# A new order table, and register loads as operations of their own, in a two-layer attention and expert kernel

## The chip, the cores and the metric

One Trainium2 chip, one of its cores. The core has five engines with queues of their own: TensorE (PE) multiplies, VectorE (DVE), ScalarE (ACT) and GpSimd (POOL) work on elements, SyncE (SP) issues transfers. Each engine runs its instructions strictly in the order in which the program lists them, and the engines wait for one another through semaphores. The metric is the device time of one execution in microseconds (us), lower is better.

## The reference

The input x has 2048 rows of 512 numbers (bf16). Two layers run one after the other, each as "x plus f(layernorm(x))" on these two functions:

```python
qkv = x @ wqkv                       # 32 heads of 16
phi = lambda t: where(t > 0, t + 1, exp(t)) + 1e-6
kv, z = sum_s phi(k) v, sum_s phi(k)
o = (phi(q) kv) / (phi(q) z + 1e-6)  # linear attention
A = o @ wo
...
r = x @ w_r                          # one score for each row
B: the 2 rows with the highest score go through silu(g @ w_gate) * (g @ w_up) @ w_down,
   are scaled by the sigmoid of their score and added back; the other 2046 rows pass through
```

The program has this A, B, A, B: attention on all rows, the expert for two chosen rows, and both again. Which two rows are chosen is known only at run time, so their indices are loaded from memory into engine registers, and copies, additions and the last transfers use these registers as addresses.

## The kernel before

The 2048 rows are 16 tiles of 128, each a [128, 512] block in SBUF. The kernel first records all its work, of both layers, as operations: each has an engine, a function that issues its instructions, and the values that it reads and writes. A string named `ORDER`, two characters for each operation, says in which order they are issued; a string `PICK` of letters (A, D, P) says which engine takes those operations that ACT, DVE or POOL could do. Nothing is reordered afterwards, so these strings are the queues. The planner's durations beside each operation (`dve(0.61, ...)`) were used when the strings were made; when the kernel is built they decide nothing. PSUM is shared out in three pools: "mm" of 3 buffers, "g" of 4 and "tp" of 1; an operation that wants a buffer waits until the reader of that buffer's last content is through.

The steps that the texts below speak of, with the line numbers before:

- **Start.** `stats` (L334, L335) is the mean and variance of a tile on DVE, `stats_act` (L348, L351) makes 1/deviation (`rho`) on ACT, L874 is a copy of a PSUM value (`wl`) on ACT, L876 (`wkc`) on DVE, L421 and L415 are the first products of keys on PE, L433 adds a tile's key-value product.
- **Side chain.** While layer 1's last tiles and layer 2's first are under way, the two chosen rows are found (L991 on PE, L996 to L1007 on DVE, which packs both indices into `pw`), loaded into POOL's registers (L1024, `load_idx`), copied out of `xn` (L1098), transposed (L1111) and put through the expert (L1069 to L1214). The second pair of loads (POOL at L1277, DVE at L1302) comes before the rows are put back.
- **Layer 2's output.** L586 is the output product, L591 adds it to x on DVE, L663 in `lin(j)` computes the score's linear part from four tiles at once (j = 0 to 3), read by DVE at L675.
- **Tail.** L681 and L684 make scores, L991, L996, L1370, L1376, L1429, L1445, L1457 and L1459 find the two best rows, L1464 makes selection weights `WL`, L1475 and L1483 select and transpose, L1491 makes `xs`, L1500 and L1540 are the expert, L1553 casts its result `yo`, L1003 and L1007 pack the indices, `regs` loads them on ACT and SP (L1024), and L1557 writes the two rows over the output. L323 and L321 make the other rows' output (`pk`), which L1360 stores in four transfers of 512 KB; the two last rows wait until all four have landed, since they overwrite rows of them.

When the operations are issued, GpSimd's that are marked `port=True` are made to wait for the last DVE instruction of that mark ahead of them in the table:

```python
if o.port and o.eng == "DVE":
    held = mine[-1]
elif o.port and held is not None:
    tc.add_manual_dep(mine[0], held.name, ...)
```

Of the kernel before, what the change touches and what calls it, by code (L numbers as in the profile page):

```python
# [28 lines left out]
ORDER = (
    "8c3y8d00010X0Y8b0302050k3z060708090P0Q0R048a0Z0a0b0S0W0V0c0T3x0U0l0e8Z0f45460g0y0w0r0i0m0h0x0n0o0z0j0p0A1I0B1D17"  # L30
    "0s0C0D1K0t101C110u12181J0v191a1U1T131L1F151b1M0E0H1E1l1c1d1A1G1B1N221e1O1Z1R1H1V421W1f1X0F1g1r1m282E2G1Y23241s1n"
    "2F1h1P1t2H1u1o2A1q2P291v251p2B26432Z2I271w341x2J2K1j0G2C2R0d2l2D3E2L2a2m0I0q2U2b2j142N162V2Q1y2k2u2S363G352T2n37"
    "2W2c0J3H2d2X401S3F2w302Y2v2e0K2f314C3Z2o2x2p3220332y2g2h2s3I3J1i2i1k383j4D3a2z3b2M3c1Q3V2O3K3N3d3P3k3l3m2q3p3W3Q"
    "3X3Y39444J3S3U4E3r3n3q4F3s3R4K3t3L4L0L3A4G8X4M4H3T413f3e3B3g3o3u3v3w4N4I3C3h1z214O4z3D4R3i4P504S514r4Q0M4d534T8Y"
    "523O4s544e4f4v4w0N4t4u552r4U2t564x4k4l3M4m4g4h4V4W4y4X4Y4j4i4748494b4c4Z4a4n4o4q575V5W58595X4A5Z4p5a5b5E5F5G5Y5S"
    "5A5B5T5U5L5M5N5O5P5D5H5o5C5p5q5r5Q5c5d5R5I6B685s5t5u5e5v6C0O5w6P5n5x5J5y6D6062665f5K6I6Q6J755g6469766R5h6X8W5i6r"
    "6W6s6y5j6z6A6K6Y5k775m617C636Z6a5l6b6c6E656L706F6M7D6d6e6f7K6G677n7o6H6t6g6N6h6j7E7u7v6S6T6n6l7p6OAC7J7LAD6p7M8P"
    "8QAE7N8I8J7O826U7w7P6u6v7Q7R8R6V83AI8K817S8f84AJA06k6w857T8gA57U6x6mAK7Y86AL7a788e7971877A888h5z8i7B6o7c89AA8j8k"
    "728A6q737W8l748B7q7r7sAM8CAgAFAh8m7V7tAi8n8E8o6i4B8p8qAB7Z8D8G7FAj7b997GAsAu8rAHAtAN7d7H7IAkAv7X8t7e7f7g7h7i9o9p"
    "9q9r7x7j8L7y7z8MAaAc80Ab7k8F8N8H7l8u8OA6A7Aw8v8s8x8w8y7mAd8z8S8T90AUAW92AG91A8A993948UAT9PAV98959Q9AAZ9B9s9C9w8V"  # L40
    "979tAX9D9u9xAf9E9y9FAe9zA19vAl9L9R9SA2A39M9H9N969G9O9I9J9K9W9TAr9UA49V9X9YAxAy9Z9aAYAmAoAn9b9dAOAP9c9eAz9f9g9hAp"
    "AqB79iB8B0AQB1BSAR9k9j9lB9B2BU9nBHBAASBRBIBJ9mCEBKBLBTB3BVBWB4B5BMBBCFBXBOCHCGBCB6BjC2BNBkBFBlBYBDC3CIBPBbBdBfBG"
    "C4CaC5BeBZBmBqBEBaBxBrBsBzBhByBnBcBQBgBtC6CRBuCJBiBpBoCdCSC0CTC1C7CKC8BvCeCOCLCWCZCXC9CMBwCYCUCfCbCgCcCsCNChCiCP"
    "CVCQCtCvCuCACjCwCyCBDACzDPCxCkCDClD0D1DBDQCmDCCnDJDMDRCoCpDDCCDFDKDND2DLDGDODEDnDHDTD3DSCrD4CqD6DUDqDrD5DtDeDoD8"
    "DuD7D9DVDWDXDfDsDpEAEBDvEMDgDaDZENDxDIECEJDyEWDwDbEKEODzDYE0DhEXDiDjDkE3DlELEYEZDmEaEQEbErE1EREsE2EPEDEtESE4EGEd"
    "EuEEEFEHEIE6EcEvEUETF0EeExEVEgEfEmEwEyEhF2DcF1DdEnF3EoEpE8EqEzEiF7E7F8EkE5EjE9FHElF9FAF5FGFKFLF4F6FIFJFBFDFNFUFC"
    "FEFRFFFMFOFPFSFQFTFVFW"
)
# [79 lines left out]
def linear_attention_moe(  # L128
# [1176 lines left out]

    def f():
# [325 lines left out]
```

## Time and profile before

| | |
|---|---|
| time, median of 3 runs | 155.57 us (155.18 to 155.70) |
| the profiled execution's own time | 155.52 us |
| its span in the trace | 153.7 us |
| mean granted clock of TensorE | 0.979 of full speed |
| PE busy | 145.5 us (95%) |
| DVE, ACT, POOL busy | 124.2, 115.8, 43.6 us (81%, 75%, 28%) |

The span is the trace's first to last record. The execution's own time is 1.8 us longer. An engine's busy time says only how often it had something to do; what an edit is worth is read at the place where it stands, from what ends the wait of whoever is waited for.

### The profile page before, as it was taken

Reading aid. Unit: us, or ns where it says so; the run is one execution under the profiler, and the core shown is the slowest. Engines: PE = TensorE matmul, PEld = TensorE weight load, DVE = VectorE, ACT = ScalarE, POOL = GpSimd, SP = SyncE. Lnnn points to the kernel's source line nnn. Section 1 sums busy time; section 2 is a strip of 40 time slices with the busy share of each in tenths; the row PEclk is TensorE's granted clock in tenths of the full one; section 3 lists DMA queues with packets and bytes.
Section 4 is the critical chain, followed back from the end, with each engine's and each line's share of the span. In section 5 each row is a group of like instructions: output and inputs, shape, how many; then the busy total and the mean of one; then the engine's idle time right before and its main releaser. Section 6 shows DMA issues by size and latency. Waiting matters only on the chain.

```text
span 153.7 us, 3661 instructions
## 1 busy us (share of the span) xinstructions
PE 145.5 (95%) x1257; PEld 71.7 (47%) x1257; DVE 124.2 (81%) x446; ACT 115.8 (75%) x276; POOL 43.6 (28%) x108
## 2 busy tenths in 40 slices
PE   7799999999999999999999999999999999995891
PEld 2344444444445444444444455445464454552480
DVE  1599998977469899999999698953759999899920
ACT  3389999888188899998899474355688988899920
POOL 7725640113000224007100002320325104786300
PEclk9999999999999999999999999999999999999965
DMA  4999999899895000531535400000000000030660
GB/s 124 349 308 389 301 234 202 113 261 346 354 384 235 0 4 0 102 37 34 105 70 95 97 17 0 4 2 0 4 0 4 0 0 0 4 136 4 210 204 1
DMA packets 23154, 18.19 MB, mean 118 GB/s; under 512 B 18016, under 2 KB 20576, under 8 KB 22752
## 3 DMA queue, kind: packets, MB, share of 16 engines
q1 hardware_dynamic: 22840, 17.57, 42.3%
q10 hardware_dynamic: 296, 0.39, 0.8%
q8 instruction: 9, 0.15, 0.4%
q14 instruction: 9, 0.07, 0.2%
HBM read 11.67 MB, written 2.10 MB: 90 GB/s over the span
## 4 chain that ended last, share of the span: by engine, by line
PE 73%; DVE 13%; ACT 5%; DMA 3%; issue 2%; POOL 1%; POOLq 0%; ACTq 0%
PE g L433 18%; PE mm L448 16%; PE mm L401 9%; PE g L586 9%; PE mm L415 9%; DVE x L591 5%; DMA x<-in_A_x_dram 3%; ACT e L370 1%; PE tp L546 1%; PE g L529 1%; PE g L1500 1%; DVE pk L323 1%; ACT rl L373 1%; PE mm L562 1%; PE mm L1069 1%
## 5 line engine op out<-in xcount | busy, mean ns | idle before, releaser
L370 ACT ACTIVATE e<-mm 128x512 bf16<-128x512 f32 x48 | 28.4, 598 | 10.3 <-PE mm L401 6.3
L448 PE MATMUL mm<-xnT,wq 128*128 128x512 bf16 x128 | 31.9, 379 | 0.0
L433 PE MATMUL g<-pk,xn 128*128 128x512 bf16 x128 | 31.1, 379 | 0.0
L586 PE MATMUL g<-KW,pq 128*128 128x512 bf16 (+2 forms) x132 | 30.0, 373 | 0.0
L606 ACT ACTIVATE sq<-x 128x512 bf16<-128x512 bf16 (+2 forms) x31 | 18.9, 609 | 1.3 <-DVE x L591 0.7
L433 PEld LDWEIGHTS <-xn 128*128 128x128 bf16 x128 | 12.4, 99 | 14.6 <-issue 0.3
L586 PEld LDWEIGHTS <-pq 128*128 128x128 bf16 x132 | 12.3, 98 | 13.7 <-DVE pq L570 0.3
L448 PEld LDWEIGHTS <-wq 128*128 128x128 bf16 x128 | 11.7, 98 | 12.8
L374 DVE TENSOR_SCALAR em<-e 128x512 bf16<-128x512 bf16 x48 | 14.1, 294 | 4.2 <-ACT e L370 4.0
L401 PE MATMUL mm<-wk,xnT 128*128 128x512 bf16 x64 | 15.8, 379 | 0.0
L415 PE MATMUL mm<-wkc,xt 128*128 128x512 bf16 x60 | 14.5, 379 | 0.0
L334 DVE BATCH_NORM_STATS2 st<-x 128x6 f32<-128x512 bf16 x16 | 10.4, 676 | 3.6 <-DMA x<-in_A_x_dram 3.6
L373 ACT ACTIVATE rl<-mm 128x512 bf16<-128x512 f32 x16 | 9.4, 594 | 3.2 <-PE mm L448 3.1
L591 DVE SCALAR_TENSOR_TENSOR x<-x,opr,g 128x512 bf16<-128x512 bf16 (+2 forms) x17 | 11.5, 708 | 0.1
L388 ACT ACTIVATE e<-mm,rho 128x512 bf16<-128x512 f32 x16 | 10.9, 687 | 0.7 <-PE mm L421 0.4
L570 POOL TENSOR_TENSOR pq<-pq,rd 128x1024 bf16<-128x1024 bf16 x2 | 4.2, 2079 | 24.3 <-DVE wor L846 15.2
L591 DVE SCALAR_TENSOR_TENSOR x<-x,g 128x512 bf16<-128x512 bf16 x16 | 10.7, 682 | 0.5 <-PE g L586 0.2
L389 ACT ACTIVATE rl<-mm,rho 128x512 bf16<-128x512 f32 x16 | 10.7, 689 | 0.5 <-PE mm L415 0.5
L381 DVE SCALAR_TENSOR_TENSOR pk<-mm,em 128x512 bf16<-128x512 f32 x16 | 10.9, 685 | 0.1
L381 DVE SCALAR_TENSOR_TENSOR pq<-mm,em 128x512 bf16<-128x512 f32 x16 | 10.8, 686 | 0.2
L323 POOL TENSOR_SCALAR xn<-x,rho,nb 128x512 bf16<-128x512 bf16 x9 | 6.8, 767 | 12.9 <-DVE em L374 4.5
L415 PEld LDWEIGHTS <-xt 128*128 128x128 bf16 x64 | 6.2, 98 | 7.5 <-issue 0.2
(297 smaller groups left out, 243.0 us busy)
## 6 DMA issues: line engine op xcount, KB each, us to landing
wgu<-in_B_wgu_dram SPq DMA_DIRECT2D x2, 1408.0 KB, 8.1
out_dram<-pk SPq DMA_DIRECT2D x4, 512.0 KB, 3.0
wd<-in_B_wd_dram SPq DMA_DIRECT2D x1, 1408.0 KB, 6.6
xt<-in_A_xt_dram SPq DMA_DIRECT2D x2, 512.0 KB, 7.7
x<-in_A_x_dram SPq DMA_DIRECT2D x2, 512.0 KB, 9.4
xt<-in_A_xt_dram SPq DMA_DIRECT2D x3, 256.0 KB, 4.4
x<-in_A_x_dram SPq DMA_DIRECT2D x3, 256.0 KB, 4.5
wq<-in_A_wq_dram SPq DMA_DIRECT2D x1, 512.0 KB
```

Source lines behind the costliest of these rows:

```text
L370: act(0.5, lambda: A.activation(out=e()[:], in_=p()[:], func=ACT.Exp), r=[p], w=[e], **k)
L373: act(0.5, lambda: A.activation(out=rl()[:], in_=p()[:], func=ACT.Relu), r=[p], w=[rl], **k)
L374: dve(0.2, lambda: V.tensor_scalar(out=em()[:], in0=e()[:], scalar1=1.0, scalar2=TINY, op0=ALU.min, op1=ALU.add), r=[e], w=[em], port=True ...
L381: dve(0.6, lambda: V.scalar_tensor_tensor(out=out_ap, in0=p()[:], scalar=0.0, in1=em()[:], op0=ALU.max, op1=ALU.add), r=[p, em], w=[key], **k)
L388: act(0.57, lambda: A.activation(out=e()[:], in_=p()[:], func=ACT.Exp, scale=s_), r=[p, ("rho0", t)], w=[e])
L401: T_.matmul(p()[:], lhsT=xnT[:, c, t * P : (t + 1) * P], rhs=wk[:, c, :], start=(c == 0), stop=(c == NC - 1))
L415: T_.matmul(p()[:], lhsT=xt[:, t, c, :], rhs=w_[:, c, :], start=(c == 0), stop=(c == NC - 1 and not raw))
L433: T_.matmul(Gs[c]()[:], lhsT=xn[:, t, gcol(c) : gcol(c) + P], rhs=pk[:, t, :], start=first, stop=last)
L448: T_.matmul(p()[:], lhsT=wq[:, i, c, :], rhs=xnT[:, i, j * D : (j + 1) * D], start=(i == 0), stop=(i == NC - 1))
L586: T_.matmul(p()[:, 0:n], lhsT=pqt(c, t * P, P), rhs=KWs[layer][:, c, a : a + n], start=(c == 0), stop=(c == NC - 1),)
L591: dve(0.07 + 0.6 * n / D, lambda a=a, n=n, p=p, h=h: V.scalar_tensor_tensor(out=x[:, t, a : a + n], in0=x[:, t, a : a + n], scalar=1.0 if ...
L606: A.activation(out=sq()[:, 0:n], in_=xh, func=ACT.Square, scale=float(D) ** -0.5, accum_out=acc)
```

## The change

The strings `ORDER` and `PICK` are replaced (966 operations in place of 963; here the first line of each):

```diff
 ORDER = (
-    "8c3y8d00010X0Y8b0302050k3z060708090P0Q0R048a0Z0a0b0S0W0V0c0T3x0U0l0e8Z0f45460g0y0w0r0i0m0h0x0n0o0z0j0p0A1I0B1D17"
...
+    "8b00010P048Z8X8Y030X028c0Q050k0607080Y090R0A0B0C0D0E0S0Z0a8a0V0H0W0F0U3x0T0l0e0G0f0h45460b0c0w0g0y0m0n0i0r0z0s17"
...
 def lin(j):
-        p, lo = ps("tp", [P, NJ, 2]), NJ * j
+        p, lo = ps("mm" if j == NC - 1 else "tp", [P, NJ, 2]), NJ * j
...
+    def load_i():
+        IV["i"], IV["t"] = load_idx(ENG.Pool, pw1)
+    pool(1.1, load_i, r=["pw"], w=["ld0"], lat=0.02)
+
     def gather():
-        IV["i"], tv = load_idx(ENG.Pool, pw1)
         for j in range(2):
-            G_.tensor_copy(out=xsel[:, j : j + 1, :], in_=xn[:, bass.ds(tv[j], 1), 0:D])
-    pool(2.2, gather, r=["pw"] + [("xn", t) for t in range(NT)], w=["xsel"], port=True)
+            G_.tensor_copy(out=xsel[:, j : j + 1, :], in_=xn[:, bass.ds(IV["t"][j], 1), 0:D])
+    pool(1.2, gather, r=["ld0"] + [("xn", t) for t in range(NT)], w=["xsel"], port=True)
...
+    def load_h():
         IV["h"] = load_idx(ENG.Pool, B["ph"], S // 2)[0]
+    pool(1.1, load_h, r=["ph"], w=["ld1"], lat=0.02)
...
+        if j == 0:
+            def load_v():
+                IV["v"] = load_idx(ENG.DVE, pw1)[1]
+            dve(0.9, load_v, r=["pw"], w=["ld2"], lat=0.02)
+
         def f(j=j, pp=pp):
-            if j == 0:
-                IV["v"] = load_idx(ENG.DVE, pw1)[1]
...
-        pl.any(first({"POOL": (0.8, False), "DVE": (0.25, True)}, eng), f,
+        pl.any(first({"POOL": (0.75, True), "DVE": (0.25, True)}, eng), f,
...
-        pl.any({"POOL": (0.55, False), "DVE": (0.27, True)}, f,
+        pl.any({"POOL": (0.5, True), "DVE": (0.27, True)}, f,
...
-           r=[("xo", t) for t in range(lo, hi)], w=[("out", lo)], lat=2.6).kb = 96.0 * (hi - lo)
+           r=[("xo", t) for t in range(lo, hi)], w=[("out", lo)], lat=2.1).kb = 96.0 * (hi - lo)
...
-    pool(0.3, f, r=["g8e", "eyg"], w=[("key", 1, NT)])
+    pool(0.42, f, r=["g8e", "eyg"], w=[("key", 1, NT)], port=True)
```

So three register loads are operations of their own, which the table can place; the last `lin` takes its PSUM buffer from "mm"; the True and False are the `port` marks, which now stand on GpSimd's small operations on scores too (`last_scales`, `halves`, and the key of L1438); the rest of the numbers are the planner's. PE's queue has 2490 rows before and after, with the same products. In the changed file the lines stand 1 to 10 further down.

Three places show how the table moves instructions. The first is SP's queue at the end of the program. L1360 (L1370 in the changed file) stores the output `pk`, L1024 (L1025) is the load of the first chosen row's index, L1557 (L1567) stores that row. Before:

```order
L1360 DMA out_dram<-pk 128x4x512 x4
L1024 TENSOR_LOAD s_194
L1024 ISA x2
L1557 REGISTER_ALU
L1557 ISA
L1557 DMA out_dram<-yo 4x128
```

Now:

```order
L1370 DMA out_dram<-pk 128x4x512 x3
L1025 TENSOR_LOAD s_194
L1025 ISA x2
L1370 DMA out_dram<-pk 128x4x512
L1567 REGISTER_ALU
L1567 ISA
L1567 DMA out_dram<-yo 4x128
```

The fourth store has moved behind the register load, which waits for the packed indices `s_194`. The second place is DVE's queue from the selection weights `WL` to the expert's input, where `s_194` is made (L1007, now L1008). Before:

```order
L1464 SCALAR_TENSOR_TENSOR WL<-keys,s_192,sc 128x45 x2
L1003 TENSOR_SCALAR s_193<-s_192 128x2
L1007 SCALAR_TENSOR_TENSOR s_194<-s_193 128x1
L323 TENSOR_SCALAR pk<-x,opr,nb 128x512 x3
L1491 TENSOR_REDUCE xs_145<-tp 128x4x2
L1491 TENSOR_REDUCE xoT<-tp 128x4x2
```

Now:

```order
L1474 SCALAR_TENSOR_TENSOR WL<-keys,s_192,sc 128x45 x2
L323 TENSOR_SCALAR pk<-x,opr,nb 128x512 x4
L1501 TENSOR_REDUCE xs_145<-tp 128x4x2
L1501 TENSOR_REDUCE xoT<-tp 128x4x2
L323 TENSOR_SCALAR pk<-x,opr,nb 128x512
L1004 TENSOR_SCALAR s_193<-s_192 128x2
L1008 SCALAR_TENSOR_TENSOR s_194<-s_193 128x1
```

The two operations that pack the indices have moved from ahead of `xs` to behind it, with one output tile more ahead of them. The third place is the start of ACT's queue. Before:

```order
L348 ACTIVATE lnv<-mv,eps_t 128x1
L351 ACTIVATE rho<-lnv 128x1
L874 ACTIVATE wl<-g 128x512
L321 ACTIVATE xn<-x,nb,rho 128x512
L388 ACTIVATE e<-mm,rho 128x512
```

Now:

```order
L967 ACTIVATE mask_102<-mask_103 128x512
L875 ACTIVATE wl<-g 128x512
L349 ACTIVATE lnv<-mv,eps_t 128x1
L352 ACTIVATE rho<-lnv 128x1
L390 ACTIVATE rl<-mm,rho 128x512
L389 ACTIVATE e<-mm,rho 128x512
```

`wl` has moved ahead of the first tile's statistics, and that tile's `xn` has left ACT (for POOL).

## Rows read from the trace of the kernel before

**Rows 1.** The page: the chain that ended last, share of the span by engine.

```profile
PE 73%; DVE 13%; ACT 5%; DMA 3%; issue 2%; POOL 1%; POOLq 0%; ACTq 0%
```

**Rows 2.** Timeline of PE, side chain: start us, us, engine, line, tiles, count.

```profile
92.07 0.38 PE L991 MATMUL tp<-identf,s 128*128 128x128 f32 x2
...
95.96 1.03 PE L433 MATMUL g<-pk,xn 128*128 128x512 bf16 x4
96.82 0.34 PE L1111 MATMUL tp<-ohm,xsel 128*128 128x2 bf16 x8
...
97.89 1.03 PE L433 MATMUL g<-pk,xn 128*128 128x512 bf16 x4
98.84 1.49 PE L1069 MATMUL mm<-wgu,xs 128*32 128x384 bf16 x32
100.26 2.76 PE L433 MATMUL g<-pk,xn 128*128 128x512 bf16 x12
```

**Rows 3.** Timeline of the start: at a row's end, idle time before it and its releaser.

```profile
6.74 0.58 ACT L874 ACTIVATE wl<-g 128x512 bf16<-128x512 f32 x1
...
7.35 1.43 DVE L876 TENSOR_TENSOR wkc<-wk,wl 128x512 bf16<-128x512 bf16 x4 [0.21 <-ACT wl L874]
7.37 1.02 PE L421 MATMUL mm<-wl,xt 128*128 128x512 bf16 x4 [0.75 <-ACT wl L874]
...
8.50 2.87 PE L415 MATMUL mm<-wkc,xt 128*128 128x512 bf16 x12
```

**Rows 4.** Timeline of PE, the last outputs and scores.

```profile
137.91 0.54 PE L663 MATMUL tp<-KWr,pq 128*128 128x2 bf16 x16
138.31 0.49 PE L586 MATMUL g<-KW,pq 128*128 128x192 bf16 x4
139.62 0.54 PE L663 MATMUL tp<-KWr,pq 128*128 128x2 bf16 x16 [0.82 <-DVE s L675]
...
141.39 0.43 PE L991 MATMUL tp<-identf,s 128*128 128x128 f32 x2 [0.78 <-DVE s L675]
```

**Rows 5.** Timeline of DVE, the same stretch and the tail.

```profile
139.48 0.40 DVE L591 SCALAR_TENSOR_TENSOR x<-x,opr,g 128x192 bf16<-128x192 bf16 x1
...
144.44 0.51 DVE L1464 SCALAR_TENSOR_TENSOR WL<-keys,s,sc 128x45 bf16<-128x45 f32 x2
...
145.13 1.05 DVE L323 TENSOR_SCALAR pk<-x,opr,nb 128x512 bf16<-128x512 bf16 x3
146.10 0.17 DVE L1491 TENSOR_REDUCE xs<-tp 128x8 bf16<-128x16 f32 x1
...
150.42 0.29 DVE L1553 CAST yo<-g 128x128 bf16<-128x128 f32 x1 [1.14 <-PE g L1540]
```

**Rows 6.** SP's queue from the fourth store; under it all four stores' landing.

```profile
146.25 0.37 SPq L1360 DMA_DIRECT2D out_dram<-pk  x1
150.73 0.70 SPq L1557 DMA_DIRECT2D out_dram<-yo  x1
...
DMA to landing us min/median/max: 3.0/3.0/3.9
```

**Rows 7.** Timeline of POOL, the copy of the chosen rows.

```profile
95.01 1.23 POOL L1098 COPY xsel<-xn 128x512 bf16 x2 [20.02 <-DVE s L1059]
```

**Rows 8.** Timeline of PE where layer 1's rows are put back.

```profile
114.56 0.22 PE L494 MATMUL g<-pk4m,V 128*128 128x128 bf16 x1
114.90 0.41 PE L546 MATMUL tp<-pq,Z 128*32 128x128 bf16 x16
```

**Rows 9.** Register loads by their line: duration ns min/median/max, first and last start.

```profile
L1024 SPq TENSOR_LOAD <-s x1: 497/497/497, 146.7 to 146.7; - x1
...
L1024 SPq SEQ_ASSERT  x1: 33/33/33, 147.5 to 147.5; - x1
```

**Rows 10.** Timeline of POOL: one small operation beside a pass of VectorE, and alone.

```profile
131.90 0.71 POOL L1341 TENSOR_SCALAR opr<-rho 128x4 f32<-128x4 f32 x1 [0.81 <-ACT rho L351]
...
135.60 0.22 POOL L1341 TENSOR_SCALAR opr<-rho 128x4 f32<-128x4 f32 x1
```

More of the change, by code (lines that the diff above doesn't have):

```diff
@@ L29 @@
 ORDER = (
-    "8c3y8d00010X0Y8b0302050k3z060708090P0Q0R048a0Z0a0b0S0W0V0c0T3x0U0l0e8Z0f45460g0y0w0r0i0m0h0x0n0o0z0j0p0A1I0B1D17"
[L31 to L44, printed above, removed]
@@ L45 @@
-    "DuD7D9DVDWDXDfDsDpEAEBDvEMDgDaDZENDxDIECEJDyEWDwDbEKEODzDYE0DhEXDiDjDkE3DlELEYEZDmEaEQEbErE1EREsE2EPEDEtESE4EGEd"
-    "EuEEEFEHEIE6EcEvEUETF0EeExEVEgEfEmEwEyEhF2DcF1DdEnF3EoEpE8EqEzEiF7E7F8EkE5EjE9FHElF9FAF5FGFKFLF4F6FIFJFBFDFNFUFC"
-    "FEFRFFFMFOFPFSFQFTFVFW"
+    "8b00010P048Z8X8Y030X028c0Q050k0607080Y090R0A0B0C0D0E0S0Z0a8a0V0H0W0F0U3x0T0l0e0G0f0h45460b0c0w0g0y0m0n0i0r0z0s17"
+    "0x0o100j0d0u0t3y1I1K0p3z1D110q0I120v151c1L1J19131a1E8d1F161C18141d1M1b1N1G281A421B1e0J1T1O1U431V1H1X1t0K1l1W1m1n"
@@ new lines @@
+    "1f2G1P292H1Z221Y2A1q2Z1u1r232E1s1v1w1R1g241Q1j1o251p1h2a2F27442I1x262B2P2j2J2K2c2b2C2D2U203E2Q3F2u2R2f3G2w3H0L2l"
+    "342v3I2V2g1i402L2k1y2x352e2d2S2m2h362y2n2W372i2X2o3Z2Y3J3a2N1k1S3b2p212T1z4C2q2s3P30383K3Q3A3R3S3N3j313T323c332z"
+    "3B3C3d3D3p4J3l3k3m3q3n3L3r0M392M4D3s3f2O4E4K3g4F3U3e3o3t3u3v4L3h413i3O4G3w2t3V4N4M4O4R4H3W4I4r4P4S4Q4d4s534t4T3X"
+    "4u543Y4U4e4v2r554f4k4V4g4w4b560N4x4h3M4y4l4z4m4j4c504Z4X515H524W4a4i5I4Y5O5J4n574o585K5E5P5S594p5F5A5Q4q5G5B5T5U"
+    "5R5L5M5Z5a5D5n5V5N5b5W5o5C5p5X475q5r5c5Y5s485d5t5u5e5f6P5v5w755x5y766I6J5g0O8W6Q5h685i69776B6K5j6R60615k626C6y7C"
@@ new lines @@
+    "66646z6X6D5l6r6A5m6Y63706Z6a7D6E6s6b67497K6c7J8P6d6F6G8Q6W657E6t8I6e6H6f6g6L6M7u4A7L7M6h8J6l8R7N7v6n6NAD8f7O6O6S"
+    "7n8K7PAP8gAE6j6TAF8h7Q7R8e6o7o7w8i6p6u6k7SAQ82A17TAR6m6q6U7U8j6V7a7p6v838k5z8l7FA67Y7cAS8485866w81717b877d8mAB8n"
+    "7G8o6x884BAJ7H728p7W8973AC7I8A7Z788r747V8tAK8B8CALAT8E8G6i8qAb7X9p797AAc9q8DAG7BAdAM9rAIAN7q9AAe7e8s7f7gAf7h9s7r"
+    "7s8FAO7i7tAH7x7y7j7k7l7m7z8S8T8L808U8v8V8M8H8N8OAn8xAoAq8u8w8y8z909192AtApAh939499959QAu9xAvAiAj9y9EA29BAU9C969R"
+    "Aa9z9798A3A09F9DA4AgAk9G9M9IAw9N9J9K9O9P9S9H9T9XAm9LA5BE9U9VA7Ar9W9YAV9tB7A89Z9a9b9u9vA9As9wAX9c9d9eAyAx9f9gAz9h"
@@ new lines @@
+    "B09i9jB49kAWB3B59mAABKBMAlAYB6B99nBAC59lBIC7BLBJCdB1AZ9oB2C6BNBOBBC0C8BUBYBPB8BXBCBZBVC1C3BmC2CHBQBnBoBWBaBSBDCI"
+    "BtC4CJCMBRBuBvCNC9BbBpBeCKCOBFBTBqBwCPBrBsBxCABgBhCBBzCQBcBGBfBiCjBHBjBkCUBdCkCRCLClCyCvBlCZByCmCVCSCcCXCWCTCYCg"
+    "CCCbCzD0CnCwChCDCxCECaCeD2DPCiD1DDCfCGCoD3D4D5CpCFDSCqDEDQD6DFDMCrDGDRDTDBCsDJDUDADNDVDWDOCuCtDXDHD7DtD8D9DuDwDq"
+    "DYDhDxEZDZDvDaDyDrDsEPDbDiDIEaEbDjDzE0EDEQEcDcDKE1EdEuEREMDLEvEEDdE2E3DkENEeDmDlDnDoEwETDpEGEIEJEFEOEHEKESE4ELDC"
+    "ExE5EyF0EXEgEfEhEjEUEVEzE6EWEiE7DfF1F2EYEqErEsEkF3DeF5F4FAEpEtFBElF6EmEnE9FKEoFCEBEAF7FLDgE8F9FDFEFFF8FGFNFHFUFJ"
@@ L48 @@
+    "FOFPFQFRECFIFSFTFVFWFXFMFYFZ"
 )
@@ L63 @@
 PICK = (
-    "DDDDADPDPPDDPDPPDDAPDDPPDDPDDDADDDDDAADAAAAADDDAPDADDAAAAADDPPAAPAAAAPPAPPAAAAPADDDDAPDADADDADDPPPDDDDPDAADAAADD"
-    "DDADDDPAPDPDADADADDAADPPPDPAAAAADPPPPPAAAAAPPPADDAAAADAAAPPDPDADD"
+    "DDDDPDPDPPDDPPPDDDPPDDPPDDDDDDPDDPDPAADDAAAADDDADPADDAAAAADDDPPPPAAAAPDPDPAAAADADDDADDDDAAPPADDDDDDDDDDDADDAAAAD"
+    "DDADDDDADDDDAPAPADDAADPPPAPPAAAADPPPPAAAAAAPDPAADDAAADAAADDDPDDAD"
 )
@@ L333, in stats @@
         st = sb("st", [P, V.BN_STATS_DIM], FP32)
-        dve(0.61, lambda: V.bn_stats(out=st()[:], in_=x[:, t, :]), r=[("x", t)], w=[st]).early = 4.0
+        o = dve(0.61, lambda: V.bn_stats(out=st()[:], in_=x[:, t, :]), r=[("x", t)], w=[st])
+        o.early, o.avail = (None, 5.4) if t == 0 else (4.0, 0.0)
         dve(0.1, lambda: V.bn_aggr(out=mv[:, 0, t, :], in_=st()[:]), r=[st], w=[("mv0", t)])
@@ L1258, in f @@
             G_.tensor_copy(out=xnT[:, :, bass.ds(IV["i"][j], 1)], in_=xc4[:, :, 2 + j : 3 + j])
-    pool(0.5, f, r=["xc4"], w=[("xnT", t) for t in range(NT)], port=True)
+    pool(0.5, f, r=["xc4", "ld0"], w=[("xnT", t) for t in range(NT)], port=True)
     qp, qe, pqx = ps("tp", [P, NC, 2]), small([P, NC, 2]), small([P, NC, 2], BF16)
@@ L1272, in linear_attention_moe @@
     dve(0.25, f, r=["qe", qp], w=["pqx"], port=True)
+    def load_h():
+        IV["h"] = load_idx(ENG.Pool, B["ph"], S // 2)[0]
+    pool(1.1, load_h, r=["ph"], w=["ld1"], lat=0.02)
     def f():
-        IV["h"] = load_idx(ENG.Pool, B["ph"], S // 2)[0]
         for j in range(2):
             G_.tensor_copy(out=pqs[0][:, :, bass.ds(IV["h"][j], 1)], in_=pqx[:, :, j : j + 1])
-    pool(0.5, f, r=["pqx", "ph"], w=[("pq", j, c) for j in range(NJ // 2) for c in range(NC)], port=True)
+    pool(0.5, f, r=["pqx", "ld1"], w=[("pq", j, c) for j in range(NJ // 2) for c in range(NC)], port=True)
     pl.bias = 4.0
@@ L1296, in linear_attention_moe @@
            r=["s2", "yw"], w=[pp])
+        if j == 0:
+            def load_v():
+                IV["v"] = load_idx(ENG.DVE, pw1)[1]
+            dve(0.9, load_v, r=["pw"], w=["ld2"], lat=0.02)
         def f(j=j, pp=pp):
-            if j == 0:
-                IV["v"] = load_idx(ENG.DVE, pw1)[1]
             xv = x[:, bass.ds(IV["v"][j], 1), :]
             V.tensor_tensor(out=xv, in0=xv, in1=pp()[:], op=ALU.add)
-        dve(0.7 + 0.9 * (j == 0), f, r=[pp], w=[("x", t) for t in range(NT)])
+        dve(0.62, f, r=[pp, "ld2"], w=[("x", t) for t in range(NT)])
     vp, vb = ps("tp", [P, 2]), small([P, 2])
```

## The prediction, made before the changed kernel ran

> **What bounds the kernel now.** I read the chain that ended last first, then the timelines at its ends and wherever it leaves TensorE. The chain is TensorE's for 73% of the span [rows 1]. From about 8.5 us on, PE issues one 128x512 matmul after another, and four of them take 0.86 us from start to start (95.96 to 96.82) [rows 2]. PE keeps this up to the last output products at 138.31, and its queue holds the same 2490 rows before and after. So a new order can win nothing between: it can only keep PE fed or make it wait. What it can win lies at two ends. At the start, L421 waits 0.75 us for `wl` [rows 3]. At the end, PE waits 0.82 us and 0.78 us for DVE, both times for the reader of a score buffer (L675) [rows 4], and then VectorE's chain and the expert's weights decide until `yo` at 150.42 [rows 5]. Close beside this end stands another: the fourth store is issued at 146.25 and lands 3.9 us later, at about 150.15, and the last row's transfer, which waits for `yo` and for the landing, starts at 150.73 [rows 5, 6]. The landing had about half a microsecond to spare. That is the number to keep in mind.
>
> **The change, part by part.** The sum is made against the profiled execution: 155.52 us, 0.05 us under the median of 155.57. I give each term a value and two ends, plus being slower.
>
> Start. ACT's `wl` moves ahead of the first tile's statistics, so L421 could start up to 0.9 us sooner. What counts is the next product, L415 at 8.50: it reads `wkc`, four passes of DVE that began at 7.35 and take 1.43 us [rows 3]. Their queue now holds a second tile's statistics ahead of them, which stood ahead before too, so they can begin about 0.6 us sooner, but the products are listed in another order and the slice that comes last is needed first by half of them; I see at most 0.3 us of gain at L415. Against it, the first tile's statistics now stand behind `wl` and a mask on ACT, and its `xn` goes to POOL: up to 0.2 us later for the first L433. Value -0.1 (-0.3 to +0.2).
>
> Side chain. From L991 to L1111 PE had 4.75 us of other work (92.07 to 96.82). Now 4 matmuls fewer lie between, so 4.75 - 0.86 = 3.89 us [rows 2]. What L1111 waits for took until 95.01 + 1.23 = 96.24, that is 4.17 us after L991 [rows 7]. The load as an operation of its own doesn't shorten that, because it still starts when the packed indices are there and the copies still follow it on POOL. So PE waits 4.17 - 3.89 = 0.3 us, in place of nothing; with another 0.3 us if the copies are held behind a DVE pass (`port`), 0.6. If DVE packs sooner, 0. Value +0.3 (0 to +0.6). Later links: the first layer-2 output product now follows four copies on ACT where one had been DVE's, and one product of the side chain has a shorter distance: +0.2 (0 to +0.6).
>
> The loads ahead of the put-back. Between 114.56 and 114.90 PE stepped 0.34 us from one matmul of 128 columns to the next, where 0.06 would do [rows 8]. DVE's own load no longer sits in that stretch. Value -0.2 (-0.3 to 0).
>
> Visits to products of 32 output rows. Where PE goes from 128 output rows to 32 and back it pays on both sides. Four L433 at 97.89 took 0.95 us until L1069 began, 0.09 more than 0.86. The 32 products of L1069, four side by side at 384 columns, should need 8 x 0.16 = 1.28 us and took 1.42 (98.84 to 100.26), 0.14 more [rows 2]. So 0.23 us a visit. The new order splits L1069 in 28 and 4 with four L433 between, and puts others of these products each by itself: by my count of PE's queue 19 visits in place of 17. Value +0.46 (+0.2 to +0.6). The Trainium skill (TensorEngine Tiling (Array Packing), Key Properties) says that changing the tiling mode drains TensorE; the trace agrees, with the 0.09 and 0.14 us here. By that rule the price is per change of mode and not per product, so that the sum for two more visits is the same +0.46.
>
> The last outputs and scores. `lin(3)` in an "mm" buffer no longer waits for the reader of `lin(2)`, and both now come after the last output product. So the 0.40 us of L663 at 137.91 to 138.31 leave the way of the last output [rows 4], and the waits of 0.82 and 0.78 us shrink or go. DVE is what follows: its last L591 was at 139.48, `WL` came 4.96 us later, `xs` 1.66 us after that [rows 5]. I expect the last L591 some 0.7 us sooner against PE's clock, since it was late by PE's 0.4 and by a queue of small operations ahead of it. `WL` follows by 0.2 less, since score work goes off PE's waits, and by 0.15 to 0.2 more at `xs`, where four output tiles stand ahead in place of three. Value for `xs`: -0.7 (-0.85 to -0.4). `yo` follows `xs` by 150.42 - 146.10 = 4.3 us as before; the expert's products don't change.
>
> The last store. SP's queue now has the register load ahead of the fourth store, and the load waits for the indices, which DVE packs only after `xs`, `xoT` and one more output tile. From `xs` that is 0.1 + 0.2 + 0.35 + 0.3 = about 0.95 us (an estimate from the spacing of the rows of DVE here [rows 5]). The load took 0.85 us on SP (146.7 to past 147.5) [rows 9], then the store is issued: 1.85 us after `xs`, in place of 0.15 (146.25 against 146.10). It lands 3.0 to 3.9 us later, and the last transfer starts about 0.2 us after that [rows 6]. So the end is at `xs` + 1.85 + 3.0 + 0.2 = `xs` + 5.0 by the store, against `xs` + 4.6 by `yo` (146.10 to 150.73). That adds 0.4 us with a landing of 3.0, and 1.3 with 3.9. Three of four stores took about 3.0, and the fourth had two others shortly ahead of it, as this one has one; I take 3.0. Value +0.4 (0 to +1.3); 0 if the store's bytes land as quickly as the planner's lower number supposes. The Trainium skill (DMA: Bandwidth & Descriptors, Anatomy of one DMA) fits a transfer on GpSimd's queue as 2.0 us plus its bytes at 436 GB/s; for 512 KB that is an estimate of 3.2 us, and by it this term would be +0.6. This store goes by SP's queue, and the trace's 3.0 to 3.9 holds the estimate.
>
> Marks on GpSimd's small operations. One that ran beside a DVE pass took 0.71 us in place of 0.22 [rows 10]. Behind the pass it begins later and runs shorter, so it ends at about the same time: 0, hidden where a tile's output is not yet waited for. If the cover is gone, a wait is one DVE pass, up to 0.5 us, inside the end of `xs` above.
>
> Sum: -0.1 + 0.3 + 0.2 - 0.2 + 0.46 - 0.7 + 0.4 = +0.36. So 155.52 + 0.36 = 155.88, and with the 0.05 to the median 155.9 us.
>
> **Rivals.** First, the tail's gain survives: the store's landing doesn't decide, and PE's stream loses only the visits. Then the terms are -0.1 + 0 + 0 - 0.2 + 0.46 - 0.7 = -0.55: 155.0 us. It decides when the landing takes less than `yo` leaves it, 4.6 - 1.85 - 0.2 = 2.55 us, or when DVE packs the indices that much sooner. For it speaks that the waits at 139.62 and 141.39 are real and removed [rows 4]; against it, that no store landed in under 3.0 us [rows 6].
>
> Second, PE starves in the side chain and the landing is the slow one: +0.6 and +0.6 there, +0.46, -0.1, -0.2, and in the tail -0.6 + 1.3. That is +2.1 at its worst; half of it, one of the two, gives +1.2 or 156.8 us. For it speaks the 3.9 us that this very store took; against it, that the packing on DVE may come sooner than in the old queue.
>
> Third, the change does nothing that can be measured because the tail is a race of two ends, and what one wins the other gives back: 155.5 us, with the visits paid by the start.
>
> **How the numbers follow.** About 0.3% (0.47 us) is what a measurement of this kernel can tell from no change. My forecast, the sum with its middle values (155.6 to 156.4), gets 0.40; the first rival 0.29; the second 0.22; the third 0.09. The first lies on the side of faster. The forecast's stretch lies to about half within 0.3% (under 156.0), the other half is slower. So faster 0.30, same 0.31, slower 0.39. The range takes the first rival down to 154.8 and the second up to 157.0.
>
> **What would show it.** In the changed trace: (1) the fourth store is issued after SP's register load, about 1.9 us behind `xs`, and SP's last transfer starts right after its landing, with `yo` done earlier; if `yo` ends last instead, the store term is wrong. (2) L1111 has a wait of 0.3 to 0.6 us for the copies on POOL; none means that the chain got quicker. (3) No wait at L663, and L991 closer behind it; `xs` at 145.4 plus what PE lost by 138. (4) PE's last output product a few tenths later than 138.31 less 0.4, by the visits and stalls. (5) L415 at 8.2 to 8.7. The prediction is wrong as a whole if PE shows waits that I have not named, above all for buffers of "mm", which `lin(3)` now shares with the scores' products.

## The result, and the profile after

The changed kernel takes 156.71 us in the median of 22 runs (156.17 to 157.80), the kernel before 156.07 us in 22 runs (155.18 to 158.03). The ratio is 1.0061, 95% interval 1.0039 to 1.0083: slower by 0.6%, about 0.95 us. Two runs of the kernel before, over 1.5% above its fastest, don't count for the ratio (the other 20 have a median of 155.95), and such runs are left out of the table and the counts below too. The forecast had the direction as the likelier one and the time in its range, but a size of 0.2% and not 0.6%. Its 155.9 us was counted from one execution of 155.52 whose clock stayed up.

The profiled execution took 157.73 us (span 155.9), one of the longer ones. Part of its length is TensorE's clock, told below; the other part is in SP's queue. VectorE's tail, as in [rows 5]:

```profile
145.31 0.51 DVE L1474 SCALAR_TENSOR_TENSOR WL<-keys,s,sc 128x45 bf16<-128x45 f32 x2
...
147.02 0.17 DVE L1501 TENSOR_REDUCE xs<-tp 128x8 bf16<-128x16 f32 x1
...
147.74 0.16 DVE L1008 SCALAR_TENSOR_TENSOR s<-s 128x1 int32<-128x1 int32 x1
...
151.21 0.29 DVE L1563 CAST yo<-g 128x128 bf16<-128x128 f32 x1 [1.14 <-PE g L1550]
```

SP's queue from the third store, as in [rows 6], then the register load and the landing by their lines:

```profile
146.52 0.37 SPq L1370 DMA_DIRECT2D out_dram<-pk  x1
149.18 0.38 SPq L1370 DMA_DIRECT2D out_dram<-pk  x1
152.91 0.71 SPq L1567 DMA_DIRECT2D out_dram<-yo  x1
...
L1025 SPq TENSOR_LOAD <-s x1: 815/815/815, 147.9 to 147.9; - x1
...
DMA to landing us min/median/max: 2.9/3.2/3.5
```

`yo` is done at 151.50, and the last row's transfer starts only at 152.91. Before, the two were 0.02 us apart. Between stand the register load, which ran from 147.9, and the fourth store, issued at 149.18, 2.16 us behind `xs`, with its landing of 3.5 us (the third store, of 146.52, took 3.5 as well). From `xs` to the last transfer it is 152.91 - 147.02 = 5.89 us; before it was 4.63 (146.10 to 150.73). There the third store had gone out at 144.21, 1.9 us ahead of `xs`:

```profile
144.21 2.41 SPq L1360 DMA_DIRECT2D out_dram<-pk  x2
```

The other part of the long execution is TensorE's clock in the tail. Granted clock (the number after the busy counts) by microsecond, PE's busy time ahead of it:

```profile
core 0: us, PE busy (x), PEclk, DMA share, GB/s
140.00:141.00 1.00, 0.40 (x2) 1.00 0.00 0
141.00:142.00 1.00, 0.62 (x3) 1.00 0.03 8
142.00:143.00 1.00, 0.65 (x3) 0.71 0.00 0
143.00:144.00 1.00, 1.00 (x15) 0.50 0.00 0
144.00:145.00 1.00, 1.00 (x18) 0.50 0.75 260
145.00:146.00 1.00, 1.00 (x5) 0.59 0.78 264
146.00:147.00 1.00, 0.74 (x26) 1.00 0.06 16
```

After two microseconds in which PE was busy 0.40 and 0.62 of the time the clock is at its lower level (1.2 GHz, 0.50) from about 142.4 to 145.8. The selection products and the fillers behind them run slower there (L1380 takes 1.09 us, in store_first below, at the higher level, 0.65), and `WL` starts at 145.31, 5.4 us behind the last L592's end (139.96); in the profile before 4.6. That is 0.8 of the 0.9 us by which `xs` is late here against [rows 5]. In every profile of this case whose clock stayed up this distance is 4.5 to 4.6 us; in the two others whose clock fell (before_lin_mm and first_lin_tp) it is 5.4 and 5.9. This isn't the change's doing: of the 22 runs of the changed kernel 8 show a mean granted clock of at most 0.972, with a median of 157.36; the other 14 have 156.51. Of 111 runs of the kernel before beside the experiments below, 40 do, at 156.29 against 155.61, which is the same share. Why it falls in one execution and not in another stays open: in store_first's profile PE was busy 0.78 and 0.26 in these two microseconds, and the clock stayed up.

PE's side chain, as in [rows 2]:

```profile
92.44 0.38 PE L992 MATMUL tp<-identf,s 128*128 128x128 f32 x2
...
96.33 0.37 PE L1115 MATMUL tp<-ohm,xsel 128*128 128x2 bf16 x8
96.56 1.02 PE L434 MATMUL g<-pk,xn 128*128 128x512 bf16 x3
97.51 1.32 PE L1070 MATMUL mm<-wgu,xs 128*32 128x384 bf16 x28
98.77 1.04 PE L434 MATMUL g<-pk,xn 128*128 128x512 bf16 x4
99.73 0.35 PE L1070 MATMUL mm<-wgu,xs 128*32 128x384 bf16 x4
100.01 1.04 PE L402 MATMUL mm<-wk,xnT 128*128 128x512 bf16 x4
```

L1115 follows L992 by 3.89 us, as worked out, and no idle time stands at it. The copies that it reads, on POOL:

```profile
95.15 1.17 POOL L1102 COPY xsel<-xn 128x512 bf16 x2 [15.33 <-DVE em L375]
```

They end at 96.32, 3.88 us behind L992 where before it was 4.17: they came just in time.

### The profile page after: what moved, and what is told of

It reads as the page before. It is cut to its first block, busy times and chain, and to the rows that moved or that the text cites. A ratio compares the mean times of both kernels' runs of the same rounds, so it can differ in the third digit from the quotient of the medians.

```text
span 155.9 us, 3645 instructions
## 1 busy us (share of the span) xinstructions
PE 146.3 (94%) x1238; PEld 72.4 (46%) x1257; DVE 127.2 (82%) x460; ACT 112.7 (72%) x271; POOL 38.7 (25%) x99
## 4 chain that ended last, share of the span: by engine, by line
PE 83%; DVE 11%; issue 2%; ACT 1%; DVEq 0%
PE mm L449 18%; PE g L434 18%; PE g L587 11%; PE mm L402 9%; PE mm L416 8%; DVE x L592 6%; PE tp L858 3%; PE tp L547 2%; PE g L530 1%; PE g L1510 1%; PE g L488 1%; DVE wkc L877 1%; PE mm L563 1%; PE mm L1070 1%; PE g L1439 1%
## 5 line engine op out<-in xcount | busy, mean ns | idle before, releaser
L449 PE MATMUL mm<-xnT,wq 128*128 128x512 bf16 x119 | 31.3, 379 | 0.6 <-issue 0.3
L434 PE MATMUL g<-pk,xn 128*128 128x512 bf16 x126 | 31.3, 379 | 0.1
L587 PE MATMUL g<-KW,pq 128*128 128x512 bf16 (+2 forms) x128 | 29.2, 372 | 0.4 <-issue 0.3
L607 ACT ACTIVATE sq<-x 128x512 bf16<-128x512 bf16 (+2 forms) x32 | 19.4, 608 | 1.4 <-DVE x L592 0.9
L434 PEld LDWEIGHTS <-xn 128*128 128x128 bf16 x128 | 12.1, 98 | 14.0 <-issue 0.7
L587 PEld LDWEIGHTS <-pq 128*128 128x128 bf16 x132 | 12.2, 98 | 13.0
L402 PE MATMUL mm<-wk,xnT 128*128 128x512 bf16 x61 | 15.8, 379 | 0.1
L375 DVE TENSOR_SCALAR em<-e 128x512 bf16<-128x512 bf16 x48 | 14.7, 311 | 1.5 <-ACT e L371 1.3
L416 PE MATMUL mm<-wkc,xt 128*128 128x512 bf16 x59 | 14.9, 379 | 0.6 <-DVE wkc L877 0.6
L592 DVE SCALAR_TENSOR_TENSOR x<-x,opr,g 128x512 bf16<-128x512 bf16 (+2 forms) x17 | 11.5, 712 | 0.3 <-PE g L587 0.3
L323 POOL TENSOR_SCALAR xn<-x,rho,nb 128x512 bf16<-128x512 bf16 x11 | 8.5, 775 | 11.4 <-ACT e L389 4.3
L592 DVE SCALAR_TENSOR_TENSOR x<-x,g 128x512 bf16<-128x512 bf16 x16 | 10.5, 682 | 0.5 <-PE g L587 0.3
L571 DVE TENSOR_TENSOR pq<-pq,rd 128x1024 bf16<-128x1024 bf16 x15 | 10.0, 686 | 0.1
L416 PEld LDWEIGHTS <-xt 128*128 128x128 bf16 x64 | 6.3, 98 | 8.0 <-issue 0.6
```

Source lines behind the costliest of these rows:

```text
L375: dve(0.2, lambda: V.tensor_scalar(out=em()[:], in0=e()[:], scalar1=1.0, scalar2=TINY, op0=ALU.min, op1=ALU.add), r=[e], w=[em], port=True ...
L402: T_.matmul(p()[:], lhsT=xnT[:, c, t * P : (t + 1) * P], rhs=wk[:, c, :], start=(c == 0), stop=(c == NC - 1))
L416: T_.matmul(p()[:], lhsT=xt[:, t, c, :], rhs=w_[:, c, :], start=(c == 0), stop=(c == NC - 1 and not raw))
L434: T_.matmul(Gs[c]()[:], lhsT=xn[:, t, gcol(c) : gcol(c) + P], rhs=pk[:, t, :], start=first, stop=last)
L449: T_.matmul(p()[:], lhsT=wq[:, i, c, :], rhs=xnT[:, i, j * D : (j + 1) * D], start=(i == 0), stop=(i == NC - 1))
L587: T_.matmul(p()[:, 0:n], lhsT=pqt(c, t * P, P), rhs=KWs[layer][:, c, a : a + n], start=(c == 0), stop=(c == NC - 1),)
```

## The experiments

All are timed in five rounds beside the kernel before, in four sets with medians of their own for it: 155.99 us (store_first, before_load_first, more_warm, both), 156.17 (pack_early, before_pair, before_lin_mm, first_lin_tp), 156.26 (before_more_warm, both_split_store, both_one_visit) and 155.88 (before_pair_later). So medians of different sets differ by some tenths without any edit; the ratio allows for that. "Low clock" counts the runs whose mean granted clock is at most 0.972.

| run | median us (runs counted) | ratio to before, 95% | low clock |
|---|---|---|---|
| changed kernel | 156.71 (22) | 1.0061 (1.0039 to 1.0083) | 8 |
| store_first | 155.84 (12) | 0.9996 (0.9967 to 1.0024) | 1 |
| pack_early | 156.33 (12) | 1.0019 (0.9988 to 1.0049) | 4 |
| before_load_first | 155.95 (10) | 1.0007 (0.9973 to 1.0042) | 3 |
| before_pair | 155.89 (11) | 0.9996 (0.9970 to 1.0022) | 5 |
| before_pair_later | 156.44 (12) | 1.0031 (0.9996 to 1.0065) | 6 |
| more_warm | 156.71 (12) | 1.0069 (1.0038 to 1.0101) | 0 |
| both | 155.73 (12) | 1.0007 (0.9983 to 1.0031) | 0 |
| before_more_warm | 155.63 (12) | 0.9963 (0.9934 to 0.9993) | 0 |
| before_lin_mm | 155.93 (10) | 0.9994 (0.9955 to 1.0033) | 4 |
| first_lin_tp | 156.73 (12) | 1.0034 (1.0002 to 1.0065) | 6 |
| both_split_store | 155.72 (11) | 0.9964 (0.9932 to 0.9997) | 0 |
| both_one_visit | 155.50 (12) | 0.9949 (0.9920 to 0.9979) | 0 |

**store_first.** Two neighbours at the end of the changed table swapped, the register loads (FX) and the fourth store (FM):

```diff
-    "FOFPFQFRECFIFSFTFVFWFXFMFYFZ"
+    "FOFPFQFRECFIFSFTFVFWFMFXFYFZ"
```

> The changed kernel with two neighbours of the table swapped, so that SP's queue has the fourth store ahead of the register load again; nothing else moves on any engine. Theory A (the store behind the late register load is what made the kernel slower): the fourth store is issued about 0.65 us behind xs in place of 2.15, has landed before yo is done, the last transfer follows yo at once, and the time falls by 0.8 to 1.3 us against the changed kernel, to between 0.2 us over and 0.5 us under the kernel before. Theory B (TensorE's clock, which fell in the tail of the profiled execution, made it slower): no change from the changed kernel, about 0.6% over before. Theory C (PE's stream before 138 us lost the time, by visits and the start): no change either.

The ratio falls from 1.0061 to 0.9996, 0.87 us in the medians. `xs`, `yo`, the fourth store and the last transfer of its profile (two timelines, DVE and SP), and its stores' landing:

```profile
146.59 0.17 DVE L1501 TENSOR_REDUCE xs<-tp 128x8 bf16<-128x16 f32 x1
...
150.94 0.29 DVE L1563 CAST yo<-g 128x128 bf16<-128x128 f32 x1 [1.14 <-PE g L1550]
...
147.26 1.19 SPq L1370 DMA_DIRECT2D out_dram<-pk  x1
151.63 0.71 SPq L1567 DMA_DIRECT2D out_dram<-yo  x1
...
DMA to landing us min/median/max: 2.9/3.5/4.2
```

The store goes out 0.67 us behind `xs`, and the last transfer follows at `xs` + 5.04 in place of 5.89. Theory A holds in the main; B and C, which expected no change, don't explain the loss. One part of A missed: the store's landing, 4.2 us, still ends last, and the last transfer starts 0.40 us behind `yo` (151.23). So the swap doesn't give back all that the store costs. Only one of these 12 runs lost the clock; among the runs that kept it the medians are 155.73 and, for the changed kernel, 156.51, 0.78 us apart.

**pack_early.** The other half undone: in the changed table the packing of the indices (code FJ) goes right behind `WL` (FC); SP keeps the load ahead of the store.

```diff
-    "...EnE9FKEoFCEBEAF7FLDgE8F9FDFEFFF8FGFNFHFUFJ"
+    "...EnE9FKEoFCFJEBEAF7FLDgE8F9FDFEFFF8FGFNFHFU"
```

> The changed kernel with the indices packed right behind the selection weights WL again, ahead of the output tiles, and the register load still ahead of the fourth store on SP. If the harm is the pair (a late packing and a store behind the load that waits for it), undoing this half alone must help like swapping the store did: the load runs about 146 to 147 us, the store is issued within 1 us of xs, and the time is 0.6 to 1.1 us under the changed kernel, 0.2% or less from the kernel before. If the place on SP alone does it, no change from the changed kernel.

```profile
146.21 0.17 DVE L1501 TENSOR_REDUCE xs<-tp 128x8 bf16<-128x16 f32 x1
...
147.07 0.68 SPq L1370 DMA_DIRECT2D out_dram<-pk  x1
150.85 0.71 SPq L1567 DMA_DIRECT2D out_dram<-yo  x1
```

The last transfer starts at `xs` + 4.64, as before the change, and the ratio is 1.0019. The median is 0.38 us under the changed kernel, less than the 0.6 to 1.1 expected, and the interval overlaps that of the changed kernel, so the time alone doesn't settle it; the rows show that the wait is gone.

**before_load_first, before_pair and before_pair_later.** The same in the old order, step by step. First only the load ahead of the fourth store on SP, with the indices packed early as ever:

```diff
-    "...F4F6FIFJFBFDFNFUFC"
+    "...F4F6FIFBFDFNFUFJFC"
```

> The kernel before with the register load ahead of the fourth store on SP, as in the change, and the indices still packed ahead of xs. If the order on SP costs by itself, 0.4 us or more slower. Theory A in its exact form (the load is late since the indices are packed late): the load runs from 145.3 to 146.2, the store is issued at 146.3 as before, and the time is the same within 0.1 us.

The same time (1.0007): the indices are there early, and the last transfer starts at 151.94, 0.02 us behind `yo`. The store itself went out later than expected, at 147.97, 0.65 us behind `xs`, since the load took 1.07 us. Then also the packing (FG), with the loads (FU) and the store (FJ), behind `xs` and `xoT` (FC):

```diff
-    "...F9FAF5FGFKFLF4F6FIFJFBFDFNFUFC"
+    "...F9FAF5FKFLF4F6FIFBFDFNFCFGFUFJ"
```

> The kernel before with only this pair put in: the indices packed behind xs and xoT, and the register load ahead of the fourth store. By the mechanism, the store is issued 1.4 to 1.7 us behind xs and lands 3.5 to 4 us later, so the last transfer starts at xs + 5.2 to 5.8 in place of xs + 4.6: 0.6 to 1.2 us slower than before (ratio 1.004 to 1.008). With a landing of 3.0, as the prediction took it, 0 to 0.2 us. If the rest of the change is what costs, no change from before.

```profile
146.53 0.17 DVE L1491 TENSOR_REDUCE xs<-tp 128x8 bf16<-128x16 f32 x1
...
148.04 0.38 SPq L1360 DMA_DIRECT2D out_dram<-pk  x1
151.16 0.71 SPq L1557 DMA_DIRECT2D out_dram<-yo  x1
...
DMA to landing us min/median/max: 2.9/3.0/3.2
```

No change (0.9996; up to 0.3 us either way is not excluded), against the 0.6 to 1.2 us that I expected first; the other case, a quick landing and 0 to 0.2 us, is what came. The store went out 1.51 us behind `xs` and took 2.9 us (the slowest of the four, with 3.2, was the third), just in time for `yo`. So the pair by itself costs nothing that shows; what counts is by how much it is late. The last of the three moves one output tile of DVE (FI) from ahead of `xs` to ahead of the packing too:

```diff
-    "...F9FAF5FGFKFLF4F6FIFJFBFDFNFUFC"
+    "...F9FAF5FKFLF4F6FBFDFNFCFIFGFUFJ"
```

> The kernel before with the pair (packing behind xs and xoT, register load ahead of the fourth store), and one of the three output tiles moved from ahead of xs to ahead of the packing as well, as the changed kernel has it. The pair alone cost nothing: the store went out 1.5 us behind xs and landed just in time. If it is the lateness behind xs that decides, not the order as such, a third of a us more must now show: the store is issued at xs + 1.8 to 2.2, lands 3.0 to 3.9 later, and the last transfer starts at xs + 5.0 to 6.2 in place of 4.6; less up to 0.3 us by which xs itself comes sooner, the time is 0.2 to 1.0 us over before. If the time is that of before again, the mechanism doesn't hold outside the changed order.

```profile
146.50 0.17 DVE L1491 TENSOR_REDUCE xs<-tp 128x8 bf16<-128x16 f32 x1 [0.23 <-PE tp L1483]
...
148.34 0.38 SPq L1360 DMA_DIRECT2D out_dram<-pk  x1
151.47 0.70 SPq L1557 DMA_DIRECT2D out_dram<-yo  x1
```

0.3 us later at the store, 0.3 us later at the end: `xs` + 4.97 in place of 4.63, and a ratio of 1.0031, in which no change is just not excluded. The landing is 2.9 us again. The mechanism works in the old order as well, with such a landing from an issue at `xs` + 1.5 on.

**more_warm, both and before_more_warm.** PE has products on zeros in its waits of the tail, with 2 and 1 matmuls in the waits before L992 and before L1380. They become 5 and 2, in the changed kernel, in store_first, and in the kernel before:

```diff
-    hot(2, [("lt", NJ - 1, NJ - 1), "Odone"], "hot1")
+    hot(5, [("lt", NJ - 1, NJ - 1), "Odone"], "hot1")
...
-    hot(1, ["tke"], "hot2")
+    hot(2, ["tke"], "hot2")
```

> The changed kernel with 5 and 2 matmuls on zeros in place of 2 and 1 in PE's waits of the tail (their results are not used, and they end before what PE waits for). Theory B: the granted clock stays at 1.00 from 140 to 147 us, the selection products (L1380, L1439) take 0.7 to 0.9 us less than in the profiled execution of the changed kernel, and the time falls by 0.3 to 0.8 us. Theory A: the clock may stay, but the store still decides the end behind xs, and the time differs by what xs gains alone, under 0.3 us in the median. Theory C: no change.

> Both of these edits on the changed kernel. Theory A: as with the store first alone, 0.8 to 1.3 us under the changed kernel. Theory B: as with more warm matmuls alone. If both hold, 1.1 us or more under the changed kernel, and below the kernel before by 0.3 us or more. Theory C: as the changed kernel.

> The kernel before with 5 and 2 matmuls on zeros in place of 2 and 1 in PE's two waits of the tail. About 4 in 10 executions of the kernels with 2 and 1 show a mean granted clock of at most 0.9725, and are about 0.7 us longer (before: 156.2 against 155.5); of 24 executions of the changed kernel with 5 and 2, none does. If that is the added matmuls' doing, no execution here does either, and the median falls to about 155.5, 0.3 to 0.5 us under the kernel before. If it was chance of those executions, 4 in 10 again and no change.

Granted clock by microsecond in the profile of more_warm, in the columns of above:

```profile
141.00:142.00 1.00, 0.69 (x5) 1.00 0.03 8
142.00:143.00 1.00, 0.85 (x6) 1.00 0.00 0
143.00:144.00 1.00, 1.00 (x24) 1.00 0.00 0
144.00:145.00 1.00, 1.00 (x19) 1.00 0.30 105
```

None of the 59 runs counted with 5 and 2 (these three kernels and the last two below) has a low clock, in the old order or the new. In the old order this is worth 0.4% (0.9963). In more_warm the median stays at 156.71: there the store decides the end. In its profile the clock stays up, the fourth store takes 4.8 us, and the last transfer starts at 153.84, 2.73 us behind `yo`; that execution took 158.56 us. So theory B names something real that both kernels have, and not the difference between them. With both edits the median is 155.73, 0.98 us under the changed kernel and 1.0007 of the kernel before; I had expected 1.1 or more, and 0.3 under the kernel before.

**before_lin_mm and first_lin_tp.** The buffer of the last `lin` by itself: "mm" in the old order, "tp" in store_first.

```diff
-        p, lo = ps("tp", [P, NJ, 2]), NJ * j
+        p, lo = ps("mm" if j == NC - 1 else "tp", [P, NJ, 2]), NJ * j
```

> The kernel before with only the buffer pool of the last lin changed to mm; the table stays. PE's wait of 0.82 us at the last L663 goes. If these waits are worth what the prediction took (0.7 us with the order around them), some of it shows here: 0.2 to 0.7 us faster. If DVE's queue of small operations decides anyway (it reads the second L663 only 0.7 us after it is done), the time is the same within 0.1 us.

> The changed kernel with the store ahead of the load, and the last lin in the pool tp again. Both L663 groups now stand back to back, so the second waits for DVE to read the first, about 0.5 us longer than with a buffer of its own. If the buffer is worth something in the new order, 0.2 to 0.6 us slower than with the store first alone (that is 155.84); if DVE decides, the same.

PE in the old order with the edit, as in [rows 4]:

```profile
138.88 0.54 PE L663 MATMUL mm<-KWr,pq 128*128 128x2 bf16 x16
...
141.47 0.65 PE L991 MATMUL tp<-identf,s 128*128 128x128 f32 x2 [1.59 <-DVE s L987]
```

The 0.82 us of wait at L663 is gone and stands at L991, which waits 1.59 in place of 0.78, and the time is the same (0.9994): DVE decides. In the new order the buffer may be worth something: without it 1.0034 against 0.9996, intervals that overlap. Among the runs whose clock stayed up the medians are 156.11 (6 runs) and 155.73 (11), 0.4 us apart, though in two sets of rounds. Half of its runs lost the clock, where one in 12 did in store_first; but the changed kernel (8 of 22) and pack_early (4 of 12) have the buffer too, so these counts don't speak for it. That the buffer is worth something is likely, not shown.

**both_split_store.** In `both`, the fourth store in two transfers, three tiles and the last one, with two output tiles exchanged in DVE's order (in the table, not shown here) so that the last tile made is the last stored.

```diff
-        op("SP", 0.42, lambda: nc.sync.dma_start(out=out_dram[:, lo:hi, :], in_=xo[:, lo:hi, :]),
+        def f():
+            for a, b in ((lo, hi - 1), (hi - 1, hi)) if hi == NT else ((lo, hi),):
+                nc.sync.dma_start(out=out_dram[:, a:b, :], in_=xo[:, a:b, :])
+        op("SP", 0.42, f,
```

> The store first and the more warm matmuls, and the fourth store in two parts: three tiles (384 KB), and the last tile (128 KB) by itself, the tile that DVE makes last. In the profiles with the store first, the last transfer still started 0.16 to 0.4 us after yo was done, since the fourth store took 3.9 to 4.2 us. If a smaller last part lands sooner, the last transfer follows yo within 0.05 us, and the time is 0.1 to 0.4 us under that of both edits (155.73), below the kernel before. If the landing doesn't depend on the size here, no change.

A miss: its last transfer starts at 150.93, 0.37 us behind `yo`, and the median is that of `both`. SP was held 1.63 us by the issue of the three tiles, so the small part went out at 147.83, and it still took 2.9 us.

**both_one_visit.** In `both`, L1070's four separate products joined to the 28: they (9L) change places with the four L434 that stood between (Am).

```diff
-    "...9H9T9XAm9LA5BE..."
+    "...9H9T9X9LAmA5BE..."
```

> The store first and the more warm matmuls, with L1070's 32 products in one visit again (the four that stood apart now ahead of the four L434 that stood between). By the price read from the trace, one visit less gives 0.2 us: from the last product of L434 before them to the first of L402 behind, PE takes 0.2 us less. The time is then 0 to 0.3 us under that of both edits. If a visit costs nothing of the end (PE's stream has slack later), the stretch is shorter and the time the same.

```profile
97.22 1.48 PE L1070 MATMUL mm<-wgu,xs 128*32 128x384 bf16 x32
98.64 1.04 PE L434 MATMUL g<-pk,xn 128*128 128x512 bf16 x4
99.52 1.03 PE L402 MATMUL mm<-wk,xnT 128*128 128x512 bf16 x4
```

From the first L1070 to the L402 behind PE takes 2.30 us, in the changed kernel 2.50 (97.51 to 100.01): 0.20 us for one visit less. The median is 155.50, 0.9949 of before, the lowest of all versions run; before_more_warm, the old order with the four matmuls alone, has 155.63 in the same rounds.

## Why the prediction was wrong

Its first point holds: the landing that had half a microsecond to spare became the end. The step that failed is a size, in "The last store": "I take 3.0. Value +0.4 (0 to +1.3)". In the profile the way from `xs` to the last transfer is 1.26 us longer, three times that and the upper end of its range. Swapping the store and the load back gave 0.87 us in the medians and left 0.40 us of waiting for the store in its profile, together again about 1.3 (an estimate). Two of its parts were taken too small. The load took 0.81 us and not 0.50, so that the store went out 2.16 us behind `xs` and not 1.85. And the landing took 3.5 us and not 3.0. The prediction counted one store shortly ahead of the fourth and still took the landing of a quick one. But the third store had moved too: it was issued 0.5 us ahead of `xs`, where in [rows 6]'s execution it was issued 1.9 us ahead, because the changed order makes its tiles later. So the fourth was issued while the third was still on its way. In the profiles here the fourth store took 2.9 us where the third had landed by then or within 0.1 us (before_pair, before_pair_later), and 3.5 to 4.8 us where it had not. I had rows at 3.0 and 3.9 and took the more frequent one; the nearest was the fourth store itself, 3.9.

That the store ahead is what lengthens a landing isn't shown. The third stores don't follow the same rule: in the six profiles of the old order they took 2.9 to 3.3 us, though issued only 1.6 to 1.8 us behind the second, which was still on its way; in the eight of the new order they took 3.5 to 4.1, in two of them (the changed kernel and first_lin_tp) with the second landed already. The cause stays open.

The other terms, point by point:

- **The sum without the store.** It was -0.04 us. store_first comes out near it: 0.9996, with an interval from 0.5 us faster to 0.4 slower. But in its profile 0.40 us of waiting for the store are still there. Without them the rest of the change is worth about -0.4 us (an estimate from that one profile), nearer the first rival's -0.55 than -0.04. So the store was taken some 0.9 us too small and the rest some 0.4 too high, and the two errors cancel in part: that the time fell in the range is partly luck.
- **Side chain, +0.3.** Wrong: no wait at L1115. The distance of 3.89 us was right, but the chain of 4.17 became 3.88: the indices were packed 1.34 us behind L992 in place of 1.51, as no `em` pass of DVE stands between the score's maximum and the packing any more, and the copies began 2.71 us behind it in place of 2.94. The further +0.2 for later links wasn't separated.
- **Loads ahead of the put-back, -0.2.** The step of 0.34 us is gone, but PE's wait there was for POOL's own load and copies (113.52 to 114.86 in the trace before), not for DVE's load. Now POOL loads the second pair at 95.3, its copies end at 113.75, and the product that reads them (L547) comes at 115.11.
- **Visits, +0.46 for two.** The price holds: 0.20 us for one, against 0.23. both_one_visit suggests that it comes off the time too: 155.50 against 155.72 for both_split_store in the same rounds (155.73 for `both` in other ones), about what PE gained, though the intervals of the two in the same rounds overlap.
- **Start, -0.1.** Not seen. The first L434 begins between 11.17 and 11.52 in the eight profiles of the changed order and between 11.07 and 11.39 in the six of the old one: some 0.1 us later in the mean. PE waited for `wkc` there (L416, 0.58 us in the profile).
- **PE's stream to the last output.** The terms up to there made +0.66. The last L587 ends at 138.7 to 139.6 in the eight, and at 138.8 to 140.0 in the six (138.31 and 0.49 more in [rows 4]), 139.1 and 139.3 in the mean; with the 0.40 of L663 moved behind it, the new order lost about 0.2 us there and not 0.66. Executions of one order differ by 1.2 us at that point, so a term of 0.3 us can't be read from one trace against one other, and this 0.2 is no better than that.
- **Tail, -0.7 at `xs`.** From the last L587's end to `xs` it is 7.04 us in store_first (139.55 to 146.59) and was 7.30 before (138.80 to 146.10); with the 0.40 of L663 that makes 0.66 us. About right, if the clock stays up. The 0.26 is what the packing's move behind `xs` brings: in pack_early it is 7.32, and in before_pair 7.04. So the move that made the store late was also the one that won here. But the waits at L663 and L991 were not the gain: in the old order they were one wait of 1.6 us for DVE, wherever it stood.
- **Marks on GpSimd, 0.** Not separated by a run, and neither were the engines that the new `PICK` gives some operations.

The first rival (the tail's gain survives) needed the landing to be quicker than 2.55 us, and no landing of these stores was. The second had the slow landing right and the starving PE wrong.

What stays open too is why SP's register load takes 0.48 to 0.50 us in most profiles and 0.80 to 1.07 in others. In the slower ones a store was moving, but it was in some of the quick ones too.

## What to carry to other kernels

A transfer that the end waits for has to be followed from the wait of what issues it: count everything ahead of it on its queue, its own operands too, since a load that waits for a late value holds all that stands behind it. Measure how much later it may come before it decides: with a landing of 2.9 us it was 1.5 us behind `xs` here, and 0.33 us more then cost 0.34; with one of 4.2, in store_first, 0.67 us was too late already. So take the landing as the range that all such transfers show (2.9 to 4.8 us here) and not as its most frequent value, and look at the clock of the executions compared before a difference of half a microsecond is put down to the change.
